# Keys and values laid channel by token, filter bins folded twice, and a new instruction order in a fused convolution and mixer kernel

## Chip, cores, metric

One core of a Trainium2 chip. The core has TensorE (PE), VectorE (DVE), ScalarE (ACT), GpSimd (POOL) and SyncE (SP), each with its own instruction queue, and 16 DMA engines. The metric is device microseconds of one execution; the profile is of one such execution.

## What is computed

The input `A_q` (2048 tokens by 640 channels) goes through two branches that a gate per token mixes. Branch A is a convolution over time: keys pass a four-tap causal filter per channel, are multiplied by the values, convolved with a filter of 2048 taps per channel (here by Fourier bins), and multiplied by the queries. Branch B is a normalized, shifted mixer and a feed-forward layer. All tensors are bfloat16.

```
x = A_q
g = sigmoid((x * gate_w).sum(-1))
# A
k_shift[t] = sum_j  k[t - j] * shift_k[:, j]          (j = 0..3)
kv = k_shift * v
y  = causal_conv(kv, ssm_k) + kv * ssm_D              (irfft(rfft(kv) * rfft(ssm_k)))
a  = q * y
# B
h  = gelu(layernorm(x) @ w1)                           (640 -> 640)
hs = [h0 shifted by +1, h1 by -1, h2 by +2, h3 by -2] @ w2
x1 = x + hs
b  = x1 + gelu(layernorm(x1) @ w3) @ w4                (640 -> 1536 -> 640)
return g * a + (1 - g) * b
```

## The kernel before

The body records operations one by one (`P.op`, `P.dma`), in program order, with the memory that each reads and writes; from that the dependences and semaphores follow. The order in which they are issued is a list of operation numbers written out by hand, `SEQUENCE`; each engine takes its own operations in that order and waits in order. `schedule` walks the list with an estimate of durations, gives each PSUM tile its bank, and adds to a load that it reckons long, not marked early and no transpose, a dependence on an earlier transfer, so that not too much is under way at once. Most operations are recorded by helpers, so they share a line: `tt` (line 669, two-tensor operations), `ts` (674, tensor with scalar), `act` (679, ScalarE), `mm` (689, matmuls), `dma` (237, and 234 for transposing ones).

**Convolution.** Time is cut into four blocks of 512 tokens, each padded to 1024 and taken to frequency bins by matmuls with constant cosine and sine matrices. A block is folded first: the second half is reversed and added to and subtracted from the first, so that even and odd parts need half the rows.

- `kv_half` and `kv_block` make keys times values for a half of the channels (`g`, 320 of 640) and a block of tokens (`b`). Tokens lie on partitions, two to a partition. Keys come with their three predecessors (`kt`, five rows of 320 a partition), so that one product with the spread taps `SHK` (128x2560) and two adds give the filtered keys; a product with `vt` follows. The reversal of tokens goes through PE with the matrix `flip` and is evicted by ScalarE (`kv_rev`); four folds of 128x640 follow. There are 16 halves and 8 blocks. `x_fwd` takes the folds to bins in `XF`: 12 matmuls of 320 columns and 4 evictions a block.
- The taps `SHK` are spread over the partitions at the start by five matmuls with `Esel`.
- `h_load`, `h_fold`, `h_chunk` do the same for the filter, 128 channels (`c`, five chunks) at a time with channels on partitions: load (`kst`), reversal on ScalarE, one fold, two DMA transposes into `het`, then 20 matmuls of 512 columns into `HF`. Bins that a fold leaves out (position 0 and 256) are added by extra matmuls with `Zn`.
- `combine` and `unit` (DVE, products of 128x2560, and accumulating DMAs of POOL) multiply the bins; `final` goes back to time with `G`, unfolds, reverses with `flip`, and multiplies by the queries.

**Mixer.** `ln1` normalizes tiles of 128 tokens (`ln_apply`; transposed by PE for the first 8 tiles, by DMA for the others), `mm1` multiplies by `w1` and applies Gelu. The last 32 channels of the four shift groups are gathered in one matmul (`ft == 4`); Gelu goes to a scratch tile `hxb`, and four DVE operations on 32 partitions each (line 924) copy it to its shifted place in `hT`. `mm2` multiplies by `w2` and adds the residual: for tiles below `RES` = 8 by a matmul with `ident`, evicted by ScalarE, for the others by DVE (line 959). `ln2` normalizes again, on DVE for tiles below `LNA` = 8, on ScalarE for the others. `mm3` and `mm4` are the feed-forward layer; `base` writes the gated residual, and later parts are added to the output by accumulating DMAs.

In the order, the filter's bins and those of keys times values are spread among the mixer's matmuls; the last forward bins (`x_fwd` of the second half) lie between the matmuls of the feed-forward layer.

## Time and profile before

| what | value |
|---|---|
| median of 3 runs (lowest, highest) | 235.31 us (234.66, 236.06) |
| profiled execution, first to last instruction | 233.8 us |
| mean granted TensorE clock | 0.994 |
| instructions: PE, DVE, ACT, POOL | 1501, 402, 317, 122 |
| transfers: packets, bytes, mean rate | 63785, 45.48 MB, 195 GB/s |
| queue 1 (issued by SP), queue 0 (issued by POOL) | 55.2%, 34.9% of the span on 16 engines |
| first matmul of `mm1` | 9.1 us |

The profiled span runs from the first to the last instruction; the device time of a run also holds what lies around it. Each row of a group gives line, engine, operation, what it writes and reads, shape and count; then, between bars, its busy time and the mean of one in ns; then the idle time of the engine just before it and what ended it. In the rows by stretch, each engine's busy us and, in brackets, its instructions stand in the order PE, weight loads, DVE, ACT, POOL; then the granted clock, the share of the DMA engines and GB/s.

### The profile page before, as it was taken

To read this page: it belongs to the slowest core of one execution; us is meant where nothing else is said; L and a number is where in the kernel's file an instruction comes from. 1 tells how busy PE (TensorE), PEld (TensorE's weight loads), DVE (VectorE), ACT (ScalarE), POOL (GpSimd) and SP (SyncE) were. 2 spreads that over 40 slices of the span, in tenths; PEclk is the share of its full clock that TensorE was granted. 3 is DMA by queue.
4 is the path that set the end of the run, shared out by engine and by line. 5 is a ranking of instruction groups with operands and counts; after the bars stand their busy time and mean duration, and the time that the engine had idled before them with its cause. 6 is when DMAs were issued, how large, how long until landed. Compare 5 with 4: busy or idle time off the path is not lost.

```text
span 233.8 us, 4171 instructions
## 1 busy us (share of the span) xinstructions
PE 221.1 (95%) x1501; PEld 134.6 (58%) x1501; DVE 220.1 (94%) x402; ACT 170.3 (73%) x317; POOL 105.9 (45%) x122
## 2 busy tenths in 40 slices
PE   7999999989998999999999999999999999999960
PEld 2598665436554656544775456654666556776630
DVE  6998999999988999998999999999989999979994
ACT  2799699488796899769949897577655387288881
POOL 0330406274495801196376693246024332456870
PEclk9999999999999999999999999999999999999997
DMA  5999959898878999978638988999978987989998
GB/s 161 360 345 250 253 146 271 246 277 204 140 181 176 240 213 317 343 212 180 157 97 145 187 189 163 146 191 206 259 142 145 196 140 142 185 98 111 95 109 165
DMA packets 63785, 45.48 MB, mean 195 GB/s; under 512 B 28818, under 2 KB 59028, under 8 KB 63764
## 3 DMA queue, kind: packets, MB, share of 16 engines
q1 hardware_dynamic: 54748, 33.33, 55.2%
q0 software_dynamic: 8832, 11.80, 34.9%
q8 instruction: 12, 0.20, 0.3%
q10 hardware_dynamic: 184, 0.08, 0.1%
q14 instruction: 9, 0.07, 0.1%
HBM read 24.22 MB, written 6.55 MB: 132 GB/s over the span
## 4 chain that ended last, share of the span: by engine, by line
PE 45%; DVE 9%; POOL 3%; ACT 2%; issue 1%
PE PSall L689 45%; DVE arena L669 8%; ACT arena L679 2%; POOL arena L674 1%; POOL arena L861 1%; POOL arena L669 1%; DVE arena L959 0%; DVE arena L674 0%
## 5 line engine op out<-in xcount | busy, mean ns | idle before, releaser
L689 PE MATMUL PSall<-arena 128*128 128x320 bf16 (+5 forms) x1444 | 213.7, 307 | 5.3 <-DVE arena L669 2.4
L669 DVE TENSOR_TENSOR arena<-arena 128x640 bf16<-128x640 bf16 (+5 forms) x247 | 182.3, 793 | 3.0 <-ACT arena L679 1.9
L689 PEld LDWEIGHTS PSall<-arena 128*128 128x128 bf16 (+1 forms) x1444 | 130.5, 98 | 86.9 <-DVE arena L669 4.2
L679 ACT ACTIVATE arena<-PSall 128x512 bf16<-128x512 f32 (+6 forms) x189 | 107.7, 634 | 29.4 <-PE PSall L689 25.2
L679 ACT ACTIVATE arena<-arena 128x640 bf16<-128x640 bf16 (+4 forms) x62 | 42.2, 703 | 6.7 <-POOL arena L669 2.7
L861 POOL TENSOR_TENSOR arena<-arena 128x1 f32<-128x1 f32 (+1 forms) x26 | 29.3, 1128 | 31.9 <-DVE arena L674 31.5
L674 POOL TENSOR_SCALAR arena<-arena 128x1 f32<-128x1 f32 (+2 forms) x41 | 24.8, 608 | 34.7 <-DVE arena L959 12.0
L237 POOL DMA_DIRECT2D out_dram<-arena x28 | 30.5, 1197 | 20.5 <-ACT arena L679 15.0
L679 ACT ACTIVATE arena<-PSall,arena 128x640 bf16<-128x640 f32 (+1 forms) x32 | 20.6, 658 | 20.0 <-PE PSall L689 19.9
L237 POOL DMA_DIRECT2D arena<-arena x12 | 14.9, 1242 | 32.1 <-DVE arena L669 28.2
L674 DVE TENSOR_SCALAR arena<-arena 128x640 bf16<-128x640 bf16 (+2 forms) x49 | 14.4, 307 | 3.4 <-POOL arena L674 1.6
L857 DVE BATCH_NORM_STATS2 arena<-arena 128x6 f32<-128x320 bf16 x32 | 14.6, 479 | 2.0 <-DMA arena<-in_A_q_dram 1.7
L669 POOL TENSOR_TENSOR arena<-arena 128x1 f32<-128x1 f32 (+1 forms) x11 | 10.3, 943 | 2.9 <-DVE arena L674 2.5
L715 PE MATMUL PSall<-arena 128*128 128x512 bf16 x15 | 5.4, 536 | 1.6 <-DVE arena L711 1.6
L959 DVE SCALAR_TENSOR_TENSOR arena<-PSall,arena 128x640 bf16<-128x640 f32 x8 | 6.4, 808 | 0.1
L924 DVE TENSOR_SCALAR arena<-arena 32x256 bf16<-32x256 bf16 (+1 forms) x24 | 5.9, 244 | 0.5
L679 ACT ACTIVATE PSall<-PSall 128x640 f32<-128x640 f32 x8 | 5.6, 699 | 0.1
L715 PEld LDWEIGHTS PSall<-arena 128*128 128x128 bf16 x15 | 1.9, 132 | 4.6 <-issue 2.5
L903 PE MATMUL PSall<-arena 128*128 128x128 bf16 x40 | 3.6, 219 | 0.3
L718 ACT ACT_TABLE_LOAD x1 | 1.3, 1283 | 2.7 <-issue 2.7
L903 PEld LDWEIGHTS PSall<-arena 128*128 128x128 bf16 x40 | 2.4, 97 | 1.4 <-DVE arena L858 0.4
L858 DVE BATCH_NORM_AGGREGATE arena<-arena 128x2 f32<-128x12 f32 x16 | 3.0, 197 | 0.0
(24 smaller groups left out, 9.6 us busy)
## 6 DMA issues: line engine op xcount, KB each, us to landing
arena<-arena POOLq DMA_DIRECT2D x12, 640.0 KB, 6.3
arena<-in_A_k_dram SPq DMA_DIRECT2D x14, 400.0 KB, 4.1
arena<-in_A_q_dram SPq DMA_DIRECT2D x14, 320.0 KB, 6.9
out_dram<-arena POOLq DMA_DIRECT2D x20, 160.0 KB, 4.2
arena<-in_A_ssm_k_dram SPq DMA_DIRECT2D x5, 512.0 KB, 4.4
arena<-in_A_v_dram SPq DMA_DIRECT2D x16, 160.0 KB, 3.9
arena<-in_B_w_dram SPq DMA_DIRECT2D x1, 1920.0 KB, 8.8
out_dram<-arena SPq DMA_DIRECT2D x10, 160.0 KB, 3.7
```

The costliest lines, as they stand in the source:

```text
L237: fn = lambda e: e.dma_start(out, in_, **kw)
L669: P.op(eng, lambda e: e.tensor_tensor(o, real(a), real(b), op), [a, b], [o], dve_ns(o, [a, b], 2) if eng == "dve" else 500)
L674: P.op(eng, lambda e: e.tensor_scalar(o, real(a), s1, s2, op0=op0, **({} if op1 is None else {"op1": op1})), [a] + aps, [o], dve_ns(o, [a] ...
L679: P.op("act", lambda e: e.activation(real(o), real(a), f, bias=bias, scale=scale, **({"accum_out": accum} if accum is not None else {})), ...
L689: fns.append(lambda e, l=l, r=r, i=i: e.matmul(real(o), l, r, start=(i == 0), stop=(i == last)))
L715: P.op("pe", lambda e: e.matmul(real(pw), warm[:, 0:128], warm[:, 128:640], start=True, stop=True), [warm], [pw], 427.0 if i < 14 else 216.0)
L857: P.op("dve", lambda e, o=o, i=i: e.bn_stats(o, i), [i], [o], 400)
L858: P.op("dve", lambda e: e.bn_aggr(bna[:, t, :], bns[k]), [bns[k]], [bna[:, t, :]], 120)
L861: P.op("pool", lambda g: g.tensor_tensor(o, a, e, ALU.pow), [a, e], [o], dur)
L903: P.op("pe", [lambda e, c=c, pb=pb, xn=xn: e.transpose(real(pb)[:, 128 * c:128 * (c + 1)], xn[:, 128 * c:128 * (c + 1)], ident) for c in r ...
L924: P.op("dve", lambda e, o=hT[q, 4, c0:c0 + n], i=hx[q, :]: e.tensor_scalar(o, i, 1.0, None, op0=ALU.mult), [hx[q, :]], [hT[q, 4, c0:c0 + n ...
L959: P.op("dve", lambda e: e.scalar_tensor_tensor(x, real(pr), 1.0, x, op0=ALU.mult, op1=ALU.add, accum_out=st[1, 0][:, t:t + 1]), [pr, x], [ ...
```

## The change

Keys and values of 128 channels are loaded by transposing DMAs from DRAM, so that channels lie on partitions and tokens along the row: `kT` holds 2048 tokens behind 16 columns of zeros, `vT` 2048 tokens. There is one buffer of each. A tap is then one scalar per partition (`wk`), and the filtered keys are four tensor-scalar products of 128x2048 that read `kT` from columns 13, 14, 15 and 16, with three adds; then comes the product with `vT`. The spreading of taps (`Esel`, five matmuls) and the loops over halves and blocks are gone.

The fold is done twice, by a helper that the filter and the products share: reversal by ScalarE within the channel's row, four DVE operations of 128x1024, and two DMA transposes. Forward bins are taken for chunks of 128 channels: 12 matmuls of 512 columns for the products, 15 instead of 20 for the filter. The three repairs of left-out bins per chunk are one-column operations on POOL, and a small copy `hsp` by SP whose row a short matmul (`Zs`) reads. The constant matrices change with this.

Gelu of the gathered channels writes straight to its four shifted places, four ScalarE operations of 32 partitions, and line 924's copies are gone. `RES` goes from 8 to 4; `LNV` (tiles normalized on DVE in `ln2`) is 4 instead of 8. The order is another list, and the banks of the PSUM tiles are a list as well (`PLACES`): the estimate of durations in `schedule`, and the dependences that it added to long loads, are gone.

In the new order all forward bins are made before the second quarter of the feed-forward layer; filter chunk 0 and a further tile pair of x are loaded ahead of `w1`; `w3`'s second part is issued by SP just ahead of the last chunk's keys, `w4` between that chunk's two value loads; 9 instead of 12 of the 16 inverse units (`final`) stand behind the last matmul of `mm4`.

```diff
-    def schedule(self, sequence, backlog=3000.0):
+    def schedule(self, sequence, places):
...
-                if o.cost > 500 and not o.tp and not o.early:
-                    gate = [(ops[d].end, d) for d in done if ops[d].end <= st]
-                    if gate:
-                        o.preds.setdefault(max(gate, key=lambda g: g[0])[1], False)
...
+    kT, vT = V(oKV, 2064), V(oKV + 2064, 2048)
+    tap = [V(oKV + 4112 + 2048 * i, 2048) for i in range(3)]
...
     const("taps")
-    for c in range(DC):
-        pr = ps(1, "set")
-        mm(pr, [(Esel[:, 128 * c:128 * (c + 1)], shk5)], guard=[V(oUT + 2048, 640)])
-        act(SHK[:, ::-1, 128 * c:128 * (c + 1)], pr.rearrange("p (d j) -> p j d", j=4), ACTF.Copy)
+    ts(wk, wkb, 1.0, None, ALU.mult)
...
+    def folds(q, rev, one, two, dst, k=None):
+        tt(one[:, 0], q[:, :, :, 0:128], rev, ALU.add)
+        tt(one[:, 1], q[:, :, :, 0:128], rev, ALU.subtract)
+        if k is not None:
+            tt(one[:, 0, :, 0, 0:1], k[:, :, 128:129], k[:, :, 384:385], ALU.add, eng="pool")
+        for e, op in enumerate((ALU.add, ALU.subtract)):
+            tt(two[:, e], one[:, :, :, 0], one[:, :, :, 1], op)
+            if k is not None and e:
+                tt(two[:, 1, 1, :, 0:1], k[:, :, 128:129], k[:, :, 384:385], ALU.subtract, eng="pool")
+            elif k is not None:
+                ts(two[:, 0, 1, :, 0:1], k[:, :, 0:1], 1.0, None, ALU.mult, eng="pool")
+            P.dma(sp, dst[:, 2 * e:2 * e + 2].rearrange("p a b c -> p (a b) c"), two[:, e].rearrange("p a b n -> p (a b n)"), transpose=True)
+
     def h_fold(c):
...
-        act(kr[:, :, 1:256], k[:, :, 511:256:-1], ACTF.Copy)
-        tt(fo[:, 1], k[:, :, 0:256], kr, ALU.subtract)
-        tt(fo[:, 0], k[:, :, 0:256], kr, ALU.add)
-        ts(fo[:, 0, :, 0:1], k[:, :, 256:257], 1.0, None, ALU.mult)
...
+        act(kr[:, :, :, 1:128], q[:, :, ::-1, 255:128:-1], ACTF.Copy)
+        folds(q, kr, kfo, kf2, het[c % 2], k)
+        P.dma(sp, hsp[c % 2].rearrange("p (a n) -> p a n", a=1), het[c % 2][0:1].rearrange("p e b c -> p e (b c)"))
...
+    def kv_load(c):
+        cs = slice(128 * c, 128 * (c + 1))
+        for h in range(2):
+            ks = slice(1024 * h, 1024 * (h + 1))
+            P.dma(sp, kT[:, 16 + 1024 * h:1040 + 1024 * h], A_k[0, ks, cs], transpose=True)
+        for h in range(2):
+            ks = slice(1024 * h, 1024 * (h + 1))
+            P.dma(sp, vT[:, ks], A_v[0, ks, cs], transpose=True)
+
+    def kv_chunk(c):
+        kv, a, b = tap
+        dst = [kv, a, b, a]
         for j in range(4):
...
+            i, w = kT[:, 13 + j:13 + j + S], wk[:, c, 3 - j:4 - j]
+            ts(dst[j], i, w, None, ALU.mult)
+            if j:
+                tt(kv, kv, dst[j], ALU.add)
+        tt(kv, kv, vT, ALU.mult)
+        q = kv.rearrange("p (b h n) -> p b h n", b=4, h=2)
+        act(xrev, q[:, :, ::-1, 255:127:-1], ACTF.Copy)
+        folds(q, xrev, xfo, xf2, xet)
...
             else:
-                hx = hxb[t0 // 256 % 2][:, 0:n]
-                act(hx, pr, ACTF.Gelu_apprx_tanh)
                 for g in range(4):
                     c0, q = 2 + SHIFT[g] + t0, slice(32 * g, 32 * (g + 1))
-                    P.op("dve", lambda e, o=hT[q, 4, c0:c0 + n], i=hx[q, :]: e.tensor_scalar(o, i, 1.0, None, op0=ALU.mult),
-                         [hx[q, :]], [hT[q, 4, c0:c0 + n]], n / 3.84 + 65)
+                    act(hT[q, 4, c0:c0 + n], pr[q], ACTF.Gelu_apprx_tanh)
...
-    RES = 8
+    RES = 4
```

257 lines of the change are left out of this document (94 added, 163 removed), and 127 rows, old and new, of tables (PLACES, SEQUENCE).

## Prediction

> **What bounds the kernel now.** I read the page first (busy shares, then the chain by engine), then the chain in order of time, the groups kept apart by shape, and the busy time by stretches.
>
> ```profile
> PE 221.1 (95%) x1501; PEld 134.6 (58%) x1501; DVE 220.1 (94%) x402; ACT 170.3 (73%) x317; POOL 105.9 (45%) x122
> ```
> ```profile
> 106.61 102.03 PE PSall L689 x640
> 208.64 0.02 issue
> 208.66 0.54 ACT arena L679
> 209.22 1.14 DVE arena L669 x2
> ```
> ```profile
> 210.00:234.00 24.00, 15.86 (x111) 10.14 (x109) 20.34 (x52) 16.35 (x32) 13.75 (x12) 0.94 0.94 118
> ```
>
> Two engines are nearly full. The chain is PE alone for 102 us, up to 208.6; the last 25 us are passed to and fro between VectorE (DVE), ScalarE and PE, and there PE is busy for 15.9 of 24 us, DVE for 20.3. So a saving counts only if both PE and DVE get it; ScalarE has 63 us to spare, GpSimd (POOL) 128.
>
> ```profile
> L669 DVE TENSOR_TENSOR arena<-arena 128x2560 bf16<-128x2560 bf16 x68 | 98.4, 1485 | 0.2
> ...
> L669 DVE TENSOR_TENSOR arena<-arena 128x640 bf16<-128x640 bf16 x80 | 36.5, 482 | 1.7 <-ACT arena L679 1.3
> L669 DVE TENSOR_TENSOR arena<-arena 128x1280 bf16<-128x1280 bf16 x44 | 35.2, 818 | 0.8 <-ACT arena L679 0.7
> ...
> L674 DVE TENSOR_SCALAR arena<-arena 128x640 bf16<-128x640 bf16 x24 | 10.2, 433 | 0.6 <-POOL arena L861 0.5
> ...
> L669 DVE TENSOR_TENSOR arena<-arena 128x1024 bf16<-128x1024 bf16 x10 | 6.7, 680 | 0.0
> L959 DVE SCALAR_TENSOR_TENSOR arena<-PSall,arena 128x640 bf16<-128x640 f32 x8 | 6.4, 808 | 0.1
> ...
> L924 DVE TENSOR_SCALAR arena<-arena 32x256 bf16<-32x256 bf16 x16 | 3.6, 222 | 0.3
> ...
> L924 DVE TENSOR_SCALAR arena<-arena 32x512 bf16<-32x512 bf16 x8 | 2.3, 287 | 0.2
> ```
>
> Between the bars stand the busy us of a group and the mean ns of one. Neighbours overlap a little: line 669's 247 instructions of 793 ns would be 195.9 us, and are busy for 182.3. So sums of DVE means are taken times 0.93. Each number below that is not worked out is a mean of these groups.
>
> A matmul's mean holds its latency; its pace is what counts. Between 198 and 204 us 47 matmuls, all of 320 columns, are busy for 6.5 us with a mean of 299 ns: (6.5 - 0.3) / 46 = 0.135 us each. For 512 columns I scale by width: 0.216.
>
> **PE, step by step.** Taps spread by five matmuls, gone: 5 x 0.216 = -1.1. Reversal of keys-times-values by `flip`, gone: 16 x 0.135 = -2.2. Filter bins: 20 matmuls per 128 channels become 15 (the even bins, 12 of the 20, need half the rows after a second fold: 7): 25 x 0.216 = -5.4. Forward bins of the products: 96 x 0.135 become 60 x 0.216, 13.0 both. Residual by `ident` for 4 tiles instead of 8: 8 x 0.135 = -1.1. Sum **-9.8**. At the head one filter load (512 KB) and a load of x (320 KB) now go ahead of `w1` on SP; at the first 20 us' 293 GB/s that is 2.8 us, and the `w1` copy (line 737) already waits 0.4 us for it. PE idles around there anyway, so 0 to 2.8, taken as **+1.5**.
>
> **DVE.** Gone: taps, 16 x (1.485 + 0.818 + 2 x 0.482) = 52.3; their folds, 32 x 0.482 = 15.4; two memsets 0.9; shifted copies of Gelu, 16 x 0.222 + 8 x 0.287 = 5.9; five bin copies 0.8; four normalizations 4 x 0.433 = 1.7. Together 77.0. New, for each of 5 chunks of 128 channels: four tap products of 128x2048, four two-tensor operations of 128x2048 and four folds of 128x1024. A two-tensor 2048 lies between 0.818 (1280) and 1.485 (2560): 1.218. A fold is 0.680. The tap product is a tensor-scalar of which no row has that length: from the copies, 0.222 at 256 and 0.287 at 512 give 0.254 ns a column, so 0.68 at 2048; from line 674, with two scalars, 0.433 + 1408 x 0.000254 = 0.79. I take 0.74. Chunk: 4 x 0.74 + 4 x 1.218 + 4 x 0.68 = 10.6, five 52.8. Filters: two more folds each, 10 x 0.68 = 6.8. Four more residual adds (line 959, with its accumulator read 0.08): 3.5. Together 63.1. Net -13.9, times 0.93: **-12.9**; with the ends of the tap product -12 to -14.
>
> Two of the four tap products read from an odd element. The shifted copies (line 924) wrote 256 columns to odd and even places, and in the timeline each took 0.20 to 0.24 us, so an odd destination costs nothing; an odd source is not shown. At the pace of line 959, the nearest row that handles one element at a time ((808 - 152) / 640 = 1.03 ns a column, 152 being a one-column operation), such a product takes 2.25 us, so the upper bound is 10 x 1.5 x 0.93 = +14. I take 0, since source and destination are streams of the same kind.
> [...]
>
> **Other engines, off the path.** ScalarE: taps -5 x 0.60, reversals -8 x 0.70, evictions of the forward bins -32 x 0.70 against 16 x 1.03 and 8 x 0.60 (the chunk that spans both halves is cut in two), reversals +5 x 1.07, Gelu in quarters (24 instead of 6: 16 x 0.40 + 8 x 0.60 - 2.8 = +8.4), residual -3, normalization +4 x 0.82: about +4, of 63 idle. Without that cover PE would wait those 4 us for PSUM. POOL: three one-column repairs per filter chunk (1.06 + 0.61 + 1.06) and four offsets: +18, of 128 idle. The second fold now waits for the first repair, with DVE's queue behind it; in the new order other DVE work stands between them in most chunks, so 0, and at most 5 x 1.1 without it.
>
> **SP and the transfers.**
>
> ```profile
> L234 SPq DMA_TRANSPOSE arena<-arena x34: 1202/1260/4504, 16.3 to 149.3; - x34
> ...
> DMA to landing us min/median/max: 2.6/3.3/7.1
> ```
>
> Gone: 36 loads of K and V at 0.58 us of SP each, -21 us of queue. New: 20 transposing loads and 10 transposes of folds at 1.26, +38, and five small copies. SP has room for +17 over 110 us, but its order is strict. The waits by which the old planner held large loads back (SP's waits for landed transfers, 3.5 us on the filter loads and 2.8 on V) are gone too: transfers may pile up. A new load is 1024 rows of 256 bytes. Its transfer costs at least SP's 1.26 us, at most queue 1's mean (54748 packets in 55.2% of 233.8 us: 2.36 ns each over 16 engines) 2.4 us: 38 to 72 us for thirty, less 16 x (640 + 256) rows of 640 bytes of K and V at 2.36 ns, 34: +4 to +38 us on queues that are busy 0.9 of the span. No row shows a transposing load from DRAM; I take the landing of 3.3 us.
>
> Does a load come in time? One buffer holds K of a chunk, so the next chunk's load goes out after the last tap product has read it. DVE work that the new order puts between, by the rows above times 0.93: about 19, 11, 10 and 5.7 us before chunks 1 to 4. The load needs 2 x 1.26 + 3.3 = 5.8 us. That fits, just, for the last: **0**, up to +4 at the largest landing seen (7.1). Behind a late load stand all of DVE's folds and products, and for them PE's forward bins.
>
> **Sum.** PE: 233.8 - 9.8 + 1.5 = 225.5. DVE: 233.8 - 12.9 = 220.9. The later is 225.5, but the tail gets denser: before, 28 us of DVE work stand behind the last down-projection matmul in the order, afterwards 14 (by the same rows), nine inverse units instead of twelve. A DVE as dense as before would reach that matmul at 208.7 again, then 14.4 x 0.93 + 1.6 of last write: 223.7. So a credit of 2 (0 to 5): **span 223.5**. The median of the runs, 235.31, is 1.5 above the profiled span, so **225.0**.
>
> **Rivals.**
> *Tail gains in full.* DVE is not the brake before the last down-projection and PE sets the time alone: 225.5 - 5 to -8 (all of PE's idle time in the last stretch): span 218.5, time 220. For it: DVE has 13.7 us of idle, with waits of 1.9 us at most. Against: both counts put DVE within 3 us of PE.
> *Loads late (slower).* If a transposing load lands after L us, chunks 2, 3, 4 lose 2.5 + L minus 11, 10 and 5.7. At L = 10 the loss is 1.5 + 2.5 + 6.8 = 10.8, the whole gain; from there it decides. At 12 it is 3.5 + 4.5 + 8.8 = 16.8: span 240, time 241.5. For it: `w3` goes out just ahead of the last chunk's load and `w4` between its values; loads of x here took up to 10.0 us; the share of the transfers is 0.94 to 1.12 in four of the first five 20 us stretches. Against: 7.1 is the most that a transpose took, and the third filter and feed-forward matmuls give PE other work.
> *Odd reads slow.* +14 on DVE: 220.9 + 14 = 235, time 236.5; the change then does not do what its cheaper taps say.
> *Gain lost in the order.* Stalls of 8 to 10 us spread over the first 100 us: about 235.
>
> **Numbers.** Forecast 0.54 (221 to 231), full tail 0.20, loads late 0.16, odd reads 0.05, lost in the order 0.05. One kernel's measurement can't tell less than about 0.5%, 1.2 us, from no change. Faster 0.74; same 0.07; slower 0.19. Range 217.5 to 237: from the full tail with some of its lower side, over the two cancelling cases, short of the late loads.
>
> **What would show it.** Right: 25 filter matmuls fewer, PE busy near 211, DVE near 207, tap products near 0.74 us whatever their start, DVE waiting for transposed loads under 4 us in all, last stretch shorter than 25 us. Wrong: tap products in two groups of 0.7 and over 1.2 us; DVE idle before tap products of chunks 2 to 4; SP's transposes of 4 us and more in number; a first projection later than 11 us.

## The result and the profile after

The changed kernel takes 243.03 us (median of four runs, 240.26 to 243.61) against 235.41 beside it: ratio 1.0287, with a 95% interval of [1.0226, 1.0347]. It is slower; 225.0 was predicted, 18 us less. Here and below a median holds all executions of a kernel, while a ratio to the kernel before leaves out those over about 1.5% above the fastest of the same kernel, and "-" stands where too few were left. The profiled execution is the fastest of the four, with a span of 238.5 us (233.8 before) and a mean granted clock of 0.961 (0.994 before).

First the page's busy us, share of the span and number of instructions for each engine of the changed kernel:

```profile
PE 218.3 (92%) x1411; PEld 128.8 (54%) x1411; DVE 209.5 (88%) x351; ACT 175.4 (74%) x315; POOL 118.6 (50%) x141
```

PE and DVE both lost busy time (2.8 and 10.6 us), yet the span grew by 4.7. So it was not more work that made it longer. The groups by shape (columns as before: busy us, mean ns, idle before):

```profile
L633 DVE TENSOR_SCALAR arena<-arena 128x2048 bf16<-128x2048 bf16 x20 | 14.5, 747 | 2.8 <-DMA arena<-in_A_k_dram 2.6
...
L628 DVE TENSOR_TENSOR arena<-arena 128x2048 bf16<-128x2048 bf16 x20 | 24.4, 1219 | 0.9 <-DMA arena<-in_A_v_dram 0.7
...
L628 DVE TENSOR_TENSOR arena<-arena 128x1024 bf16<-128x1024 bf16 x40 | 26.5, 683 | 2.5 <-DMA arena<-arena 2.0 <-ACT arena L638 0.4
```

The three new durations came out at 747, 1219 and 683 ns; 740, 1218 and 680 had been taken. The tap products from odd and even columns take the same: all twenty lie between 704 and 789 ns.

The chain of waits in order of time (start, us, what), from 62 us on, its transfers and PE's long pieces:

```profile
64.14 4.82 DMA arena<-in_A_k_dram
...
73.76 3.98 DMA arena<-arena
77.74 0.14 issue
77.88 15.26 PE PSall L648 x70
...
95.92 5.72 DMA arena<-in_A_k_dram
...
108.94 3.53 DMA arena<-arena
112.47 0.14 issue
112.61 111.75 PE PSall L648 x698
```

From 112.6 us the chain is PE alone to 224.4, as before, and the rest is 14 us long instead of 25. What is new stands ahead of it: the chain passes through transfers, loads of keys and transposes of folds. SyncE's (SP's) transposes, with the shortest, middle and longest time of one on its queue in ns:

```profile
L235 SPq DMA_TRANSPOSE arena<-arena x44: 1205/1276/4592, 18.6 to 186.6; - x44
L235 SPq DMA_TRANSPOSE arena<-in_A_k_dram x10: 1181/1464/3127, 8.5 to 95.9; - x10
L235 SPq DMA_TRANSPOSE arena<-in_A_v_dram x10: 1298/1510/5630, 16.9 to 101.1; - x10
...
DMA to landing us min/median/max: 2.6/3.9/9.8
```

The twenty loads keep SP for 40.0 us in sum, 2.0 each. In the timeline of SP between 66 and 78 us (start, us) two fold transposes of chunk 1 lie among the six of the first row:

```profile
66.20 8.88 SPq L235 DMA_TRANSPOSE arena<-arena x6
75.14 2.67 SPq L235 DMA_TRANSPOSE arena<-in_A_k_dram x2
```

The second of the two had its data at 65.56 us and went out last, at 73.76, behind two transposes of `ln2` that nobody read until 99.7. It landed at 77.74, and PE began at 77.88. By stretch (busy us of PE, weight loads, DVE, ACT, POOL; clock; DMA share; GB/s):

```profile
70.00:74.00 4.00, 4.00 (x21) 1.78 (x20) 4.00 (x6) 3.82 (x8) 0.00 (x0) 1.00 0.90 168
74.00:78.00 4.00, 0.63 (x3) 0.23 (x3) 3.97 (x6) 1.59 (x4) 1.97 (x2) 0.84 1.02 176
78.00:82.00 4.00, 4.00 (x12) 1.64 (x11) 0.97 (x2) 1.96 (x3) 1.52 (x4) 0.50 1.00 244
```

PE idles for 3.3 us and then works for four at half the clock (0.81 is the mean of the next four), with 12 matmuls where 21 went in the four before the hole. Busy time hides this, so the runs below are compared by **lost PE time**: the moment t less the time that all matmuls started before t need at full pace (0.216 us for 512 columns, 0.136 for 320, 0.109 for 256, as the starts of matmuls behind one another lie apart in the traces of before and after; others in proportion, but 0.03 for a single column, whose starts lie 0.025 us apart).

| lost PE time (us) at t = | 20 | 45 | 70 | 90 | 110 | 125 | 220 |
|---|---|---|---|---|---|---|---|
| before | 4.9 | 5.8 | 7.1 | 8.1 | 8.6 | 8.5 | 9.1 |
| after | 11.6 | 13.2 | 15.5 | 22.7 | 23.2 | 24.2 | 24.1 |
| s1_sp | 12.3 | 13.6 | 15.0 | 17.7 | 26.6 | 26.7 | 34.7 |
| s3_spj | 12.0 | 14.0 | 16.6 | 21.9 | 27.9 | 28.0 | 29.0 |
| s4_head | 6.9 | 8.5 | 15.3 | 20.3 | 22.5 | 24.7 | 24.7 |
| p2_plain | 6.9 | 7.7 | 12.4 | 13.5 | 15.0 | 15.6 | 16.1 |

The work at full pace fell from 216.2 to 206.3 us. Against before, 7.4 us are lost by 45 us, 7.2 more by 110, then almost none. The head's part shows in PE's timeline (start, us, and in brackets the idle time before). The first row is the first matmul of `mm1` before; the two others are the first transposes and the first matmul of `mm1` in after:

```profile
9.13 0.72 PE L689 MATMUL PSall<-arena 128*128 128x128 bf16 x10
10.55 1.01 PE L865 MATMUL PSall<-arena 128*128 128x128 bf16 x15 [3.74 <-DVE arena L633]
12.67 2.31 PE L648 MATMUL PSall<-arena 128*128 128x128 bf16 x20 [1.11 <-ACT arena L638]
```

From 12 to 18 us the granted clock is 0.50 in after and 1.00 before. Three questions follow: what loses the head, what the middle, and why the median lies 2.8 us above this run.

### The profile page after: what moved, and what is told of

Read it like the earlier page. It is cut to its first block, busy times and chain, and to the rows that moved or that the text cites. A ratio compares the mean times of both kernels' runs of the same rounds, so it can differ in the third digit from the quotient of the medians.

```text
span 238.5 us, 3908 instructions
## 1 busy us (share of the span) xinstructions
PE 218.3 (92%) x1411; PEld 128.8 (54%) x1411; DVE 209.5 (88%) x351; ACT 175.4 (74%) x315; POOL 118.6 (50%) x141
## 4 chain that ended last, share of the span: by engine, by line
PE 60%; DVE 15%; DMA 11%; ACT 8%; SPq 3%; issue 1%; DVEq 0%
PE PSall L648 59%; ACT arena L638 8%; DVE arena L628 8%; DMA arena<-arena 5%; DMA arena<-in_A_k_dram 4%; DVE arena L633 4%; SPq L235 2%; DMA arena<-in_A_q_dram 2%; DVE arena L918 1%; DVE arena L812 1%; PE PSall L865 1%; SPq L238 1%; DVE arena L813 0%; DVEq L364 0%
## 5 line engine op out<-in xcount | busy, mean ns | idle before, releaser
L648 PE MATMUL PSall<-arena 128*128 128x320 bf16 (+4 forms) x1354 | 211.0, 316 | 9.3 <-DMA arena<-arena 4.1
L648 PEld LDWEIGHTS PSall<-arena 128*128 128x128 bf16 x1354 | 124.6, 100 | 95.2 <-ACT arena L638 7.6
L628 DVE TENSOR_TENSOR arena<-arena 128x2560 bf16<-128x2560 bf16 (+6 forms) x201 | 163.7, 861 | 9.7 <-ACT arena L638 4.7
L638 ACT ACTIVATE arena<-PSall 128x512 bf16<-128x512 f32 (+8 forms) x182 | 105.0, 625 | 27.9 <-PE PSall L648 21.9
L638 ACT ACTIVATE arena<-arena 128x640 bf16<-128x640 bf16 (+4 forms) x75 | 53.6, 741 | 16.2 <-POOL arena L628 9.1
L633 POOL TENSOR_SCALAR arena<-arena 128x1 f32<-128x1 f32 (+3 forms) x46 | 35.2, 770 | 19.9 <-DVE arena L813 11.1
L816 POOL TENSOR_TENSOR arena<-arena 128x1 f32<-128x1 f32 (+1 forms) x26 | 26.0, 1011 | 36.3 <-DVE arena L633 35.8
L633 DVE TENSOR_SCALAR arena<-arena 128x1 f32<-128x1 f32 (+3 forms) x61 | 26.3, 453 | 4.1 <-DMA arena<-in_A_k_dram 2.6
L628 POOL TENSOR_TENSOR arena<-arena 128x1 f32<-128x1 f32 (+2 forms) x25 | 16.8, 680 | 24.1 <-DVE arena L628 23.6
L918 DVE SCALAR_TENSOR_TENSOR arena<-PSall,arena 128x640 bf16<-128x640 f32 x12 | 9.8, 820 | 7.2 <-PE PSall L648 7.0
L865 PEld LDWEIGHTS PSall<-arena 128*128 128x128 bf16 x40 | 2.6, 104 | 3.9 <-DVE arena L633 3.8
L675 PEld LDWEIGHTS PSall<-arena 128*128 128x128 bf16 x15 | 1.8, 126 | 4.4 <-issue 2.2
```

Source lines behind the costliest of these rows:

```text
L628: P.op(eng, lambda e: e.tensor_tensor(o, real(a), real(b), op), [a, b], [o], dve_ns(o, [a, b], 2) if eng == "dve" else 500)
L633: P.op(eng, lambda e: e.tensor_scalar(o, real(a), s1, s2, op0=op0, **({} if op1 is None else {"op1": op1})), [a] + aps, [o], dve_ns(o, [a] ...
L638: P.op("act", lambda e: e.activation(real(o), real(a), f, bias=bias, scale=scale, **({"accum_out": accum} if accum is not None else {})), ...
L648: fns.append(lambda e, l=l, r=r, i=i: e.matmul(real(o), l, r, start=(i == 0), stop=(i == last)))
L675: P.op("pe", lambda e: e.matmul(real(pw), warm[:, 0:128], warm[:, 128:640], start=True, stop=True), [warm], [pw], 427.0 if i < 14 else 216.0)
L816: P.op("pool", lambda g: g.tensor_tensor(o, a, e, ALU.pow), [a, e], [o], dur)
```

## Experiments

Each run has its times (median, lowest to highest) and its ratio to the kernel before, which took 235.3 to 235.8 us beside them.

| run | us | ratio |
|---|---|---|
| m1_merged | 243.33 (241.15-245.60) | 1.025 [1.0196, 1.0304] |
| h1_head | 244.93 (244.08-248.22) | 1.0383 [1.0331, 1.0435] |
| g1_gelu | 247.10 (244.00-248.35) | 1.0421 [1.0329, 1.0514] |
| w1_warm | 244.17 (241.82-249.89) | 1.0329 [1.0256, 1.0402] |
| p1_plain | 240.02 (239.47-241.39) | 1.0201 [1.0154, 1.0248] |
| f1_fill | 243.81 (241.89-247.67) | 1.0316 [1.0262, 1.037] |
| n1_lnv | 243.82 (239.71-244.41) | - |
| o1_order | 260.69 (258.82-265.20) | 1.1043 [1.0959, 1.1127] |
| s1_sp | 250.05 (248.51-251.34) | 1.0612 [1.0558, 1.0667] |
| s2_spln | 250.73 (249.07-253.18) | 1.0621 [1.055, 1.0691] |
| s3_spj | 243.80 (242.50-245.22) | 1.0334 [1.0265, 1.0403] |
| s4_head | 240.95 (238.97-242.25) | 1.0202 [1.0121, 1.0284] |
| p2_plain | 233.05 (231.78-233.88) | 0.9873 [0.9797, 0.9949] |
| q1_pool | 247.51 (241.76-251.41) | - |
| a2_acts | 243.50 (243.28-245.15) | 1.0314 [1.0247, 1.0382] |
| b1_mload | 240.37 (239.84-240.81) | 1.0166 [1.0105, 1.0226] |
| b2_mfold | 243.84 (242.28-244.13) | 1.0299 [1.0219, 1.0379] |
| p3_vplain | 234.59 (234.28-236.09) | 0.9964 [0.993, 0.9998] |

### First round: four parts of the change

**m1_merged**: K and V of a chunk in one transposing load each, ten instead of twenty.

```diff
-        for h in range(2):
-            ks = slice(1024 * h, 1024 * (h + 1))
-            P.dma(sp, kT[:, 16 + 1024 * h:1040 + 1024 * h], A_k[0, ks, cs], transpose=True)
+        P.dma(sp, kT[:, 16:2064], A_k[0, :, cs], transpose=True)
...
+        P.dma(sp, vT, A_v[0, :, cs], transpose=True)
```

> Each pair of transposing loads of keys, and of values, is one load of 2048 rows: 10 instead of 20, same bytes, nothing else moved. Theory S (SP is too slow: from 38 to 92 us it issues without a pause, and a transpose costs it 1.2 to 1.3 us whatever its size): SP saves some 12 us before 92 us, PE's idle 3.3 us before 77.9 us and the half clock after it go, DVE's 2.65 us for keys at 69 us goes; time down by 5 to 7 us, to 236 to 238. Theory H (head and ScalarE set the early stage): within 1 us of 243. [...]

The time stayed, and so, nearly, did SP's: 37.4 us for ten loads against 40.0 for twenty. So the cost went more with the bytes than with the instructions. In the profiled execution, with 245.60 us the slowest of the four, lost time at 90 us fell by 3.3 us (19.4 against 22.7), and came back later. Where, POOL's timeline of m1_merged shows (start, us, and in brackets the idle time before):

```profile
116.13 6.01 POOL L812 TENSOR_TENSOR arena<-arena 128x1 f32<-128x1 f32 x1 [4.56 <-DVE arena L633]
```

and DVE's, over the same time:

```profile
115.71 0.33 DVE L633 TENSOR_SCALAR arena<-arena 128x1 f32<-128x1 f32 x2
115.96 5.76 DVE L628 TENSOR_TENSOR arena<-arena 128x1280 bf16<-128x1280 bf16 x5
```

A one-column operation on POOL took 6.01 us (1.07 is the mean of its group in after), as long as a run of five two-input products on DVE that started ahead of it; it ended at 122.14, the five at 121.72. A normalization on ScalarE waited 3.8 us for POOL, and PE 3.2 us for ScalarE. The same operation took 6.02 us in g1_gelu, and in p1_plain ScalarE waited 4.1 us for POOL between 108 and 130 us.

**h1_head**: the load of `w1` ahead of the filter's, tile 0 first on PE; DVE's order left as it was.

```diff
-SP: x0 x0 x0 x0 x1 h0 x1 w1 w1 x2
+SP: x0 x0 x0 x0 x1 w1 w1 x1 h0 x2
```

> Order of the head alone: w1 ahead of the filter load on SP, PE takes tiles 0, 1, 2 in the order in which DVE normalizes them, the first matmuls of mm1 are those of tile 0, ScalarE reverses the filter after tile 2. Theory H (PE lost 7 us against the kernel before by 20 us, by waiting for tile 2 first and by the halved clock after that): first matmul of tile 0 near 8.2 us, granted clock above 0.95 in the first 20 us, time down by 5 to 7 us. Theory G (ScalarE, with Gelu in quarters, is full from 19 to 35 us): PE gains at the head and loses it again by 35 us, time down by 0 to 1.5 us. Theory S: no more than 1 us, as SP is late by itself.

No gain: 11.9 us lost at 20 us against 11.6. The wait only changed its place. A one-column filter operation stands in DVE's queue ahead of a normalization and now waited 2.25 us, until 13.15, for the filter's load. Here the load could not be moved alone; who reads it had to move too.

**g1_gelu**: the four quarter Gelus undone.

```diff
-                    act(hT[q, 4, c0:c0 + n], pr[q], ACTF.Gelu_apprx_tanh)
+                hx = hxb[t0 // 256 % 2][:, 0:n]
+                act(hx, pr, ACTF.Gelu_apprx_tanh)
+                    P.op("dve", lambda e, o=hT[q, 4, c0:c0 + n], i=hx[q, :]: e.tensor_scalar(o, i, 1.0, None, op0=ALU.mult),
```

> Gelu of the gathered channels undone: one ScalarE operation of 128 partitions and four DVE copies, as in the kernel before, at the same places of the order. ScalarE has 18 operations fewer (some 8 us), DVE 24 more (5.9 us). Theory G: ScalarE's full stretch from 19 to 35 us shortens by 5 us, time down by 3 to 5 us. Theory H or S: the early stage is not ScalarE's; time within 1 us of 243, or 1 to 2 us longer by DVE.

Not faster but 4.1 us slower than after by the medians, so undoing the quarters wins nothing. Its trace has the late POOL delay too (6.02 us at 119.5), and 4.2 us are lost between 125 and 135 us.

**w1_warm**: 16 more of the matmuls that keep PE busy before the first real one.

```diff
-        P.op("pe", lambda e: e.matmul(real(pw), warm[:, 0:128], warm[:, 128:640], start=True, stop=True),
+        P.op("pe", [lambda e: e.matmul(real(pw), warm[:, 0:128], warm[:, 128:640], start=True, stop=True)] * (1 if i < 14 else 17),
```

> 16 more warming matmuls at the end of the 15, so that PE is busy from 1.6 to about 10 us; nothing that the output needs is later. It parts the clock from the wait: if the half clock from 11.7 to 17.5 us is what the head loses, clock in the first 20 us goes from 0.83 to above 0.95 and time falls by 2.5 to 3.5 us; if ScalarE's evictions or the loads pace PE there, clock rises and time falls by under 1 us.

The clock is 1.00 over the first 20 us instead of 0.83, for about 1 us at the head and nothing in the whole. Half clock at the head (0.50 in after, behind 3.74 us without a matmul) went with the idle time and is not the cause.

### Second round: loads, the hole, ScalarE's part, the order

**p1_plain**: the twenty loads plain, 128 rows of 2048 bytes, no transposition.

```diff
-            P.dma(sp, kT[:, 16 + 1024 * h:1040 + 1024 * h], A_k[0, ks, cs], transpose=True)
+            P.dma(sp, kT[:, 16 + 1024 * h:1040 + 1024 * h], bass.AP(A_k.tensor, A_k.offset + 131072 * (2 * c + h), [[1024, 128], [1, 1024]]))
```

> The twenty loads of K and V are plain copies of the same number of bytes to the same places, 128 rows of 2048 bytes each; the transposition is left out, so the products are of other elements. Theory S (the transposing loads fill SP's queue and the transfers behind it: in the changed kernel SP spent 40.0 us on them, 2.0 us each, and was busy back to back from 8.5 to 62 us and again to 92): a plain load takes SP 0.6 us, so some 28 us of its queue go; PE's 3.3 us hole before the last forward bins of chunk 1 and the half clock behind it go, PE's lost time between 70 and 90 us falls from 7.2 to under 2, the time from 243.0 to about 235 (232 to 238). Theory C (what is lost is lost in the head and by the clock, whatever the loads do): 241 to 244, lost time between 70 and 90 us still over 5. Theory P (chance delays of GpSimd's small operations behind long products on VectorE, after 110 us): no change of its own, the spread of the runs stays at 3 us or more.

3 us better in the median. By 110 us it lost about 17 us against 23.2 (its trace lacks 15 matmuls, 8 of them before 110 us; they are counted in here); part went again behind late waits of ScalarE, 5 us between 115 and 125. The run changes the length of the rows together with the transposition.

**f1_fill**: 14 matmuls without use ahead of chunk 1's last bins, to keep the clock through the hole at 74.6 us.

```diff
+            if (c, j) == (1, 3):
+                P.op("pe", [lambda e, pr=pr: e.matmul(real(pr)[:, 0, :], ident, V(oR, 512), start=True, stop=True)] * 14, ...)
```

> Fourteen matmuls of 512 columns, whose result is overwritten, stand ahead of the last forward bins of chunk 1, where PE was idle for 3.28 us at 74.6 us and then ran at half clock for 6 us (76 to 82). Theory C (an idle hole of over 3 us halves the granted clock behind it, and this costs about 3 us more): the granted clock stays 1.00 from 70 to 90 us, the bins that took 0.59 to 0.63 us take 0.38, and PE's lost time between 70 and 90 us falls from 7.2 by about 3 (filler counted as lost); time 240 if nothing behind it waits. Theory S: the clock is restored, but the transfers are as late as before, so PE waits elsewhere before 92 us and the time stays at 241 to 244.

The clock held (1.00 from 70 to 90 us) and the time stayed: PE waited elsewhere, 3.2 us for ScalarE between 108 and 130 us.

**n1_lnv**: tiles 4 to 7 of `ln2` normalized on DVE, as before the change.

```diff
-    LNV = (range(NT), range(4))
+    LNV = (range(NT), range(8))
```

> The second normalization of tiles 4 to 7 is applied on VectorE again, as before the change, so GpSimd's four offset products and four of ScalarE's waits for GpSimd go; everything else, its order too, stays. Theory P (GpSimd's one-column operations stand behind runs of long two-input products on VectorE, 6.0 us for tile 6's power in two of five profiles, and ScalarE's queue behind them): ScalarE's waits for GpSimd fall from 9 to under 6 us, no loss of 3 us or more for PE between 115 and 135 us, the spread of the runs narrows and the median falls by 1 to 3 us, to 240 to 242. Theories S and C: no change of the median beyond 1 us, 242 to 244; VectorE has 4 x 0.43 = 1.7 us more.

Between 115 and 135 us nothing was lost, as the theory of late POOL waits has it; but the profile of after loses nothing there either, so this does not confirm it. At 155 to 185 about 3 us were lost, where ScalarE waited 5.0 us for a transpose. The median stayed.

**o1_order**: the same operations in another list and with other PSUM places, made from estimated durations.

> The very same operations and transfers, each on its own engine and in its own buffers; only the order of every engine's queue and the PSUM places are others, worked out with 2.3 us of transfer time for a transposing load and a half clock behind idle holes of 2.5 us. If the change's own operations set the time (S in its strong form: so many transposing loads can't be fitted in), it stays at 240 or above. If it is the order that was given with them (the loads would fit, but SP's queue holds what PE needs next behind what is needed later), PE's lost time at 90 us falls from 22.7 to 15 or less, and the time to 230 to 236.

The estimate was wrong (half clock behind 2.5 us of idle time was part of it; after shows half clock with idle stretches of 3.74 and 3.28 us), and the run says nothing about a good order. It does say what order is worth: 17.7 us more than after with not one operation changed.

### Third round: SP's order

**s1_sp**: SP's operations from 60 us on by the time at which they are needed.

```diff
-SP: ln2.1 x1 h3 ln2.0 h3 x1 K3 K3 w3 ... x2 x2 w3 ln2.3
+SP: x1 h3 V2 x1 h3 ln2.0 ln2.1 ... w3 w3 ln2.2 x2 x2 ln2.3
```

(`x1`, `x2`, `h3`: transposes of the folds of product chunks 1, 2 and filter chunk 3.)

> Only the order of SP's queue is another, from 60 us on: of what is ready, the transfer whose first reader comes soonest goes first. In the changed kernel the second transpose of chunk 1's folds was ready at 65.56 us and went out at 73.76, behind two transposes of the second normalization that nobody read before 99.7 us and two loads of V with 13 us to spare; the transposes of chunk 3's folds went out 5 and 7 us late behind the last load of V, which held SP for 5.63 us behind w4. Theory S in the form that the order of SP's queue makes PE wait (its total would fit): the hole of 3.3 us at 74.6 us and the half clock behind it go, PE's lost time at 110 us falls from 23.2 to 17 or 18, time 237 to 240, since the delays after 110 us stay. If the transfers themselves are too slow in any order (the strong form), lost time at 110 us stays at 21 or more and the time at 241 to 244.

The hole at 74.6 us was gone: 5.0 us less lost at 90. Then a larger one opened, here by stretch (columns as above):

```profile
85.00:90.70 5.70, 5.70 (x29) 2.44 (x26) 3.84 (x6) 4.80 (x5) 0.00 (x0) 1.00 0.70 181
90.70:97.90 7.20, 0.00 (x1) 0.03 (x1) 2.37 (x2) 1.12 (x2) 0.00 (x0) 0.73 1.16 285
```

and in SP's timeline:

```profile
86.45 1.08 SPq L238 DMA_DIRECT2D arena<-in_B_w_dram x2
87.58 9.51 SPq L235 DMA_TRANSPOSE arena<-arena x4
```

Both parts of `w3` (1920 KB) went out together, and chunk 2's fold transposes behind them were held at 3.32 and 2.95 us on SP. PE stood still for 7.2 us. In after, `w3`'s larger part went out behind these transposes.

**s2_spln**: s1 with `LNV` of n1, and tile 12's square later on ScalarE.

> As the run before, and besides: the second normalization of tiles 4 to 7 is applied on VectorE again, and the square of tile 12, which writes its unused result over a buffer that the transpose of tile 10 reads, goes later in ScalarE's queue (with what follows from it on VectorE and GpSimd), since ScalarE waited 4.6 to 5.3 us for that transpose in four of seven profiles. Theory S with P: both late losses go, PE's lost time stays within 1 us from 115 to 220 us, time 233 to 236, spread of the runs under 2 us. Theory S alone: as the run before within 1 us, 237 to 240. If the delays after 110 us only move to another place as soon as PE comes earlier (VectorE, which was full from 120 to 200 us, sets the pace there), PE's lost time rises again by 3 us or more between 115 and 190 us and the time stays at 238 or more.

The same hole. No loss at 115 to 135; 6.4 us are lost at 175 to 185, behind ACT's longest wait for a transfer (view of waits: us in total, times, longest):

```profile
ACT arena L640 <- DMA arena<-arena: 7.6, 1, 7.6
```

ScalarE's squares write an unused result over a buffer that a transpose of `ln2` still reads, and ScalarE waited 7.61 us, until 178.73, for that transpose. What held it back was not shown.

**s3_spj**: `w3`'s larger part behind chunk 2's transposes; `LNV` of n1; the unused squares of tiles 8 to 15 to a place of their own.

```diff
-        act(xn2[t % 2], X[:, t, :], ACTF.Square, scale=D ** -0.5, accum=st[1, 1][:, t:t + 1])
+        act(xn2[t % 2] if t < 8 else V(oKV + 4608, 320).bitcast(mybir.dt.uint8), X[:, t, :], ACTF.Square, scale=D ** -0.5, accum=st[1, 1][:, t:t + 1])
```

> SP's order again, mended by what the run with SP's order showed (5.0 us gained up to 90 us, then 7.2 us lost because both parts of w3 went out ahead of chunk 2's fold transposes, which SP held for 3.3 and 3.0 us): chunk 1's and chunk 2's fold transposes go before the loads of V and the transposes of the second normalization, the larger part of w3 behind chunk 2's. Besides, tiles 4 to 7 are normalized on VectorE again, and the unused result of the squares of tiles 8 to 15 goes to a place that no transpose reads. Theory S with P: PE's lost time at 110 us falls from 23.2 to 18 or less and rises by less than 2 us from there to 220 us; time 233 to 237, spread under 2 us. If the transfers are too slow in any order, a hole of 3 us or more opens before another chunk's bins (2, 3 or 4), and the time stays at 240 or above.

Late losses are gone: 27.9 us at 110, 29.0 at 220. But between 85 and 110 new waits took what was won; the middle shifts its loss from one reader of a transpose to the next.

**s4_head**: s3 with a new head: `w1` ahead of the filter's load, the taps' many short rows last in ScalarE's queue, tile 0 first on PE, and the filter's fold later on DVE.

```diff
-SP: x0 x0 x0 x0 x1 h0 x1 w1 w1 x2 w2 x2 K0 K0
+SP: x0 x0 x0 x0 x1 w1 x1 w1 h0 w2 x2 x2 K0 K0
```

> As the run before, and in the first 44 us the order of the changed kernel's queues is given up: w1 goes ahead of the first filter load, the taps' load of 640 short rows goes last on ScalarE's queue, the filter fold waits behind the first tiles on VectorE, and PE begins with tile 0. Theory H (the head's loss, 11.6 us at 20 us against 4.9 before the change, is one of order: the filter's and the taps' loads ahead of w1, PE waiting for tile 2 first, and the half clock behind the wait): lost time at 20 us falls to 8 or less, at 45 us from 13.2 to 9.5 or less, and, with SP's order mended, the gain is still there at 220 us: time 229 to 233. If SP's queue or the transfers bind up to 90 us whatever the head does, lost time at 90 us is within 1 us of the run before and so is the time.

First matmul of `mm1` at 9.7 us (12.7 in after, 9.1 before), 8.5 us lost at 45 instead of the 14.0 of s3. Against after, where 13.2 were lost at 45 us and 5.8 before the change, that is 4.7 of 7.4: about two thirds of the head's loss is order. Which of the four moves does it was not separated. The middle did not move: 14.0 us between 45 and 110. The largest entry of PE's waits (us in total, times, longest):

```profile
PE PSall L650 <- DMA arena<-arena: 7.7, 7, 2.6
```

Seven short waits for fold transposes; SP is never idle for over 1 us between 14 and 101.

### Fourth round: what fills SP's queue

**p2_plain**: s4 with the twenty loads plain, as in p1_plain.

> The run with the head's order, its twenty loads of K and V made plain copies of the same bytes (the transposition is left out). There the head's gain held to 45 us (8.5 us lost against 14.0) and the late losses stayed away (24.7 at 125 and at 225 us), but between 45 and 110 us 14.0 us were lost, with SP never idle for over 1 us from 14 to 103 us and seven waits of PE for landed transposes. Theory S: the transposing loads are what fills SP's queue there; PE's lost time at 110 us falls from 22.5 to 12 to 15 and the time to 230 to 234. If something else sets that stage (VectorE, ScalarE, the other transposes), it stays at 20 or more and the time at 239 to 242.

233.05 us: 7.9 less than s4, and the only run over 1% under before, with the transposition left out. PE's waits for transposed folds:

```profile
PE PSall L650 <- DMA arena<-arena: 1.6, 1, 1.6
```

and SP's issues of the loads (shortest, middle, longest in ns):

```profile
L238 SPq DMA_DIRECT2D arena<-in_A_k_dram x10: 421/509/752, 7.4 to 86.5; - x10
L238 SPq DMA_DIRECT2D arena<-in_A_v_dram x10: 328/584/1529, 10.3 to 88.8; - x10
```

The same bytes keep SP for 12.1 us instead of 37.9. The middle stretch of s4:

```profile
45.00:110.00 65.00, 55.80 (x288) 26.08 (x287) 53.69 (x90) 47.32 (x71) 24.81 (x37) 0.97 1.00 202
```

and of p2:

```profile
45.00:110.00 65.00, 60.37 (x327) 29.34 (x326) 59.14 (x98) 53.38 (x82) 31.70 (x37) 1.00 0.90 211
```

39 more matmuls in the same 65 us, all other engines denser too, and the share of the transfers down from 1.00 to 0.90. So p2_plain relieves two things at once: SP's queue, and the DMA engines. By the packet records, the twenty transposing loads of s4 are 20480 packets of 256 bytes and take about 31.5 us of all 16 engines, the plain ones 2560 packets of 2048 bytes and 16.8 us.

By these figures the transposing loads were not as fast as plain ones in long rows, neither on SP (37.9 us for 12.1) nor on the 16 engines (31.5 for 16.8). No run copies plainly in rows of 256 bytes, so short rows are a rival to the transposition. Against it: transposes within SBUF, which read no short rows of DRAM, also move in packets of 256 bytes (25600 of them before, with a median of 18 ns, as for all 56320 in after), and in after a fold transpose of 256 KB took SP 1.23 us at the least, a transposing load 1.18.

**q1_pool**: s4 with 15 plain transfers issued by GpSimd.

```diff
-        P.dma(sp, w4, B_w4.rearrange("(c p) f -> p c f", p=128))
+        P.dma("pool", w4, B_w4.rearrange("(c p) f -> p c f", p=128))
```

> The run with the head's order; all transposing loads stay, but fifteen plain transfers (four filter loads, five of the filter's first row, the bin matrices, one of x, w3 and w4) are issued by GpSimd instead of SP: 9.5 us of SP's time less between 14 and 103 us, and no transpose stands behind w3 or w4 in the same queue. If SP's strict queue is the limit (its instructions, and what holds them behind large loads), lost time at 110 us falls from 22.5 to 16 to 19, the time to 234 to 238. If the limit is the transfers themselves (the 16 engines or the transposition), whoever issues them, it stays at 21 or more, the time at 239 to 242. If GpSimd is delayed by the issues or its queue is held up by a wait, ScalarE's and VectorE's waits for GpSimd grow and the time is over 242.

GpSimd itself became late (its waits for DVE reach 8.3 us in the profiled execution, the slowest of the four), and the times scatter over almost 10 us; the run says nothing on SP.

**a2_acts**: s4 with 11 plain transfers on ScalarE's queue (`w3`, `w4`, late filter loads, `hsp`).

```diff
-        P.dma(sp, w4, B_w4.rearrange("(c p) f -> p c f", p=128))
+        P.dma("act", w4, B_w4.rearrange("(c p) f -> p c f", p=128))
```

> The run with the head's order; all transposing loads stay on SP, but eleven plain transfers from 34 us on (two filter loads, five of the filter's first row, a bin matrix, w3 and w4) go out on ScalarE's queue, each at a place where ScalarE had a gap: 6.6 us of SP's time less, and no transpose stands behind w3 or w4 in the same queue (those were held for 2.8 to 3.7 us). If SP's strict queue is part of the limit, PE's lost time at 110 us falls from 22.5 to 17 to 20 and the time from 241.0 to 236 to 239. If only the transposing loads' transfers count (7.9 us by the run with plain loads), it stays at 21 or more, 240 to 242.

Slower, and SP's time on the twenty loads rose from 37.9 to 44.9 us. Fewer instructions in SP's queue did not empty it: over the first 110 us SP's issues took 103.2 us, 102.4 in s4.

**b1_mload** (a2 with m1's merged loads) and **b2_mfold** (a2 with one transpose instead of two for each pair of folds):

```diff
-            P.dma(sp, dst[:, 2 * e:2 * e + 2].rearrange("p a b c -> p (a b) c"), two[:, e].rearrange("p a b n -> p (a b n)"), transpose=True)
+        P.dma(sp, dst.rearrange("p a b c -> p (a b) c"), two.rearrange("p e a b n -> p (e a b n)"), transpose=True)
```

> As the run before, with the two transposing loads of K and of V of a chunk merged to one each (ten of 512 KB instead of twenty of 256 KB). If SP's cost is per instruction, another 5 us of its time go (1.65 us was the shortest merged load, 2.6 two single ones) and the time falls by 1 to 3 us more, to 234 to 237; if the cost goes with the bytes (37.4 us for ten, 40.0 for twenty, in the first merged run), it stays within 1 us of the run before.

> As the run with eleven plain transfers on ScalarE, with the two fold transposes of each chunk and each filter chunk merged to one (ten of 512 KB instead of twenty of 256 KB): the first half waits for the second fold, 0.7 to 1.3 us on VectorE. If the cost is per instruction, 5 to 9 us of SP's time go and PE's lost time at 110 us falls by 2 to 4 us more, time 234 to 237; if it goes with the bytes, the later landing of the first half costs PE 1 us at each of ten chunks that it waits for, and the time rises by 1 to 4 us.

b1 is 3 us faster than a2 and level with s4; its ten loads took SP 32.6 us, the twenty of a2 44.9. Here merging did pay, other than in m1. b2 is level with a2: ten merged fold transposes took 26.2 us, twenty 33.3. In all three runs halving the number saved far less than half (7, 27 and 21%), so here most of the cost went with the bytes, and a part with the instructions.

**p3_vplain**: s4 with V's ten loads alone plain.

```diff
-            P.dma(sp, vT[:, ks], A_v[0, ks, cs], transpose=True)
+            P.dma(sp, vT[:, ks], bass.AP(A_v.tensor, A_v.offset + 131072 * (2 * c + h), [[1024, 128], [1, 1024]]))
```

> The run with the head's order, with only V's ten loads made plain copies of the same bytes (V's transposition is left out), K's ten stay transposing. If what is lost goes with the transposed bytes in the queue, half of the 7.9 us between that run (241.0) and the one with all loads plain (233.1) comes back: 236 to 238, lost time at 110 us 18 to 20. If it is K's loads, whose single buffer gives them the least time, that PE waits for, V's change nothing: 240 to 242, 22 or more. If any relief of the queue is enough, it comes to 233 to 235.

234.59 us. Half of the transposed bytes, those with the most time to spare, gives back 6.4 of the 7.9 us by the medians, 2.4 of 3.3 points by the ratios. PE's lost time at 110 us is about 17 (with 8 matmuls that its trace lacks counted in), against 22.5 in s4 and 15.0 in p2. That is less like a price per load than like something that was full, where the first relief ends most of the waits. That this is SP's queue alone does not follow: over the first 110 us SP's issues took 96.3 us here, and 94.0 in b1 and 95.9 in b2, which gained nothing on s4.

No version with all transposing loads came under before; b1_mload is the best, 2.7 us under after. Transposes issued from two queues were not tried.

## Why the prediction was wrong

The profiled span was to be 223.5 and is 238.5 us. The 15.0 us between them are, from the table of lost time: work at full pace 0.1 less than taken (-9.9 for -9.8), the head 5.9 more (7.4 less the 1.5 taken), the middle 7.2, 110 to 220 us 0.4, and the tail's credit of 2 of which 0.4 came, 1.6. The median adds 3.0 more: it lies 4.5 above the profiled span, where 1.5 was taken.

**PE's and DVE's sums: right, nearly.** PE's work fell by 9.9 us for 9.8; that PE is busy for 218.3 us and not near 211 goes with its clock (a mean of 0.961 for 0.994). DVE's durations added up fell by 13.3 us for 13.9, but its busy time by 10.6 for 12.9, as neighbours overlap less. 747 ns for 740. Odd reads cost nothing, as taken: all twenty tap products took 704 to 789 ns, where 2.25 us was the upper bound. DVE waited 3.3 us for the loads of K and V (under 4 expected), 2.65 of it once, ahead of chunk 2's first tap product, and 2.0 more for transposes of folds.

**The head, "+1.5 ... PE idles around there anyway": wrong.** It counted the bytes ahead of `w1` and not the order of those who read them. The first matmul of `mm1` came at 12.7 us, 3.5 later (over 11 was a sign of being wrong), PE idled 3.7 us on the way, and worked at half clock afterwards: 7.4 us by 45 us. s4_head took 4.7 of them back by order alone.

**"SP has room for +17 over 110 us": the step that failed in the middle.** It priced a load at 1.26 us, the median of transposes within SBUF (their mean was 1.50). Measured: 2.0, 40 us for twenty instead of 25. The upper bound of 2.4, named for the transfers, was near; SP's sum went by the lower. Over the first 110 us SP's issues grew from 75.7 us to 103.6, by 28 instead of 17. SP was then back to back from 8.5 to 93 us, but for one pause of 0.5, and its strict order, named in the same sentence, did the rest: late were loads and the fold transposes behind them. On the chain shown above they stand with 10.5 us (two loads of K) and 7.5 us (two fold transposes).

**"Does a load come in time? ... 0, up to +4": wrong in a part of its object.** It asked if a load comes in time for DVE. Part of the price appeared there, but PE's waits name transposed folds, which stood in the same queue (4.1 us in after, 7.7 in s4_head). p2_plain prices the whole at 7.9 us. The rival "loads late" (241.5) had the time nearly right by luck: it takes a landing of 12 us, and the longest of all transposes was 9.8, the median 3.9. Nearest in kind was the rival "gain lost in the order", at a chance of 0.05: stalls of 8 to 10 us spread over the first 100. Measured at 110 us are 14.6 more than before; of these another order gave back 4.7 at the head and, in the runs tried, nothing that lasted in the middle.

**ScalarE, POOL and SP "off the path" at no cost: in part wrong.** Their totals leave room (POOL 118.6 of 238.5), but two waits of theirs cost 3 to 5 us in m1_merged, g1_gelu and n1_lnv: POOL's one-column operation beside DVE's products (6.01 us in m1_merged), ScalarE's squares over a buffer in use (5.0 us of waiting in n1_lnv). s3_spj and s4_head, with both changed, lose 1 us or less from 125 to 220. As h1_head and w1_warm, without either change, also lose nothing between 115 and 135, chance may have a part in it. The profiled run of after shows neither; that they are the 2.8 us between it and the median is likely and not shown.

**The tail: right in kind.** 14 us instead of 25 stand behind the last long run of PE, with DVE busy for 9.4 of them instead of 21.1; but the span is PE's work plus its losses, and of the credit of 2 us only 0.4 came.

Open: whether the brake in the middle is SP's issuing or the DMA engines that serve it. SP's time per load and the share of the transfers between 45 and 110 us went together in p2_plain (0.6 us, 0.90), s4_head (1.9, 1.00) and a2_acts (2.2, 1.05), though not in every run (2.1 and 0.96 in o1_order). a2_acts speaks against the number of instructions, m1 and b2 for the bytes; b1 and b2, with SP as much relieved as in p3_vplain and no gain on s4, speak against SP's issuing as the only brake. No run puts back the dependences by which the old planner held large loads. p2_plain still loses 15.0 us by 110 where before lost 8.6; what of it the order can give back was not found.

## What to carry to other kernels

When work moves from PE and DVE to transposing loads, the queue that issues them is an engine with a sum of its own (here 40.0 us of SP for twenty loads), and its transfers have another (31.5 us of the 16 engines in s4_head): price each load by its bytes in both, put every operation of that queue in one line, and ask what stands behind a held one. Where such a sum is full, half of the relief can bring most of the gain, as in p3_vplain (6.4 of 7.9 us). And compare kernels by work at full pace, not by busy time, since in after 3.28 us of idle time came with 7.2 us of lost time between 70 and 90.

## What was not expected of the hardware

- After 3.28 us without a matmul (after, at 74.6 us), PE's granted clock was 0.50 for the next 4 us: the lost time grew by 7.2 us between 70 and 90, of which the wait was 3.3. It is not so each time: behind another 3.28 us, at 112.5 in b2_mfold, the clock stayed at 1.00.
- A transposing load of 256 KB in rows of 256 bytes held SP 2.0 us on average (up to 5.6) in after, a plain load of the same bytes in rows of 2048 held it 0.6 in p2_plain; merged to 512 KB, 3.7 in m1_merged and 3.3 in b1_mload.
- Transposes behind large plain loads were held on SP: 3.32 and 2.95 us instead of the median of 1.28, behind 1920 KB (s1_sp).
- A one-column GpSimd operation took 6.01 us instead of 1.07 beside five DVE products in a row (m1_merged).
